# Loads of the second MoE's w_out paced by a one-column copy from the first MoE's values

## The chip, the cores and the metric

The kernel runs on one core of a Trainium2 chip. The metric is the device time of one launch in microseconds; the kernel before has a median of 1230.97 us over 3 runs (1230.19 to 1234.41). Engines are called as the profile calls them: PE is TensorE (PEld its weight loads), DVE is VectorE, ACT is ScalarE, POOL is GpSimd, and SP is the engine whose queue issues the DMAs. TensorE's clock has two levels, 1.2 and 2.4 GHz; the profile's PEclk gives the granted share of full speed.

## The reference

The program is an attention with a bias made of relative positions, followed by two MoE-like feed-forward layers:

```python
def reference(...):
    # attention: q, k, v are (4, 8, 576, 64)
    scores = q @ k^T / 8 + bias(w1, b1, w2)     # bias: relu(x @ w1 + b1) @ w2 of log distances
    attn = softmax(scores); x = (attn @ v) laid out as 2304 tokens x 512
    # first MoE, 512 -> 1536 -> 512
    g = x @ w_gate; val = x @ w_val
    x = (g * sigmoid(g) * val) @ w_out
    # second MoE, 512 -> 2048 -> 512
    h = maximum(x @ w_in, 0)
    return (h * h) @ w_out
```

The inputs that matter here are float64 weights, which the kernel decodes itself.

## The kernel before, in words

**Precision.** Matmuls run in float16. Every operand is split into a high and a low half, and a product takes three matmuls (high x high, high x low, low x high). The weights are float64 in memory: a block of 128 rows x 512 columns (512 KB) is loaded as it is, decoded on DVE into float32 by three instructions (`decode`, L262, L265, L267), its norm is taken, and once a common scale is known, each block is split into halves (`split`, `halves`): either POOL makes the high half (L197) and DVE the low one (L191), or ACT scales and casts (L205, L209) and POOL subtracts (L220).

**Two streams.** The program is written by two generators whose instructions are interleaved while it is emitted. Stream "a" holds the attention and the preparation of weights (`first`, `second`, `weights2`). Stream "m" holds the first MoE, in nine units of 256 tokens (`moe1(m)`, m = 0 to 8). Each `yield` of a number adds that much to the stream's position, and the loop at the end goes on with "m" when "a" is ahead of it by the table `LEAD`, else with "a". A scheduler with a timeline model then decides the final order on each engine.

**The first MoE.** A unit goes through 12 columns f. For each, 24 matmuls (L458) fill a PSUM tile with gate and value, ACT takes the tanh, and DVE forms `th` in two instructions (L467, L469), which also empty the PSUM tile. Three PSUM tiles are in turn (tags `mm` twice, `ma` once). ACT casts `th` to the high half of `zx`, POOL subtracts for the low half (L220). Then 2 x 36 matmuls (L481) make two output tiles of 128 tokens; `out_y` (L491 to L501) normalizes them and stores them.

**The second MoE's w_out** (key "2"). `weights2` calls `second(..., later=True)` for its 16 blocks. Three raw rooms (`w2s`) take turns. Each block is loaded by SP (L283), decoded by DVE, and its square norm goes to ACT. After each block the next load is issued into the room that came free, and the generator yields 1.6. After the last block, DVE and two small matmuls (L139 and L169) turn the norms into a scale, and the 16 splits follow one after the other. Blocks f and 8+f are then combined (`combine`, sums of L1193 and casts of L1200) for the Strassen-like products of the later units.

**The second MoE.** `plain(0)` treats unit 0 alone: layer 1 is 16 tiles of 12 matmuls (L1378), each followed by relu and square (L1383, L1387) and by the split of the result (L1198 for the cast on DVE), layer 2 is two output tiles of 48 matmuls (L1406). Five of the eight `combine` calls are written among `plain(0)`. Then come four pairs of units, (1,2) to (7,8), each with a layer 1 of 8 column steps (`hidden`: matmuls, relu and square, differences by POOL, halves) and products (`outputs`, L1450). The lines of the program are those before the change; in the changed program they stand 4 or 5 further down from the class `Source` on.

Of the kernel before, what the change touches and what calls it, by code (L numbers as in the profile page):

```python
# [10 lines left out]
F32 = mybir.dt.float32  # L11
# [5 lines left out]
ALU = mybir.AluOpType  # L17
# [58 lines left out]
def tile_attention_moe(  # L76
# [4 lines left out]
    nc = tc.nc  # L81
# [20 lines left out]
    st = {}  # L102
# [3 lines left out]
    def keep(n=1):  # L106
        sc_n[0] += 1
        return res.tile([P, n], F32, name=f"keep{sc_n[0]}")
# [3 lines left out]
    def scr(shape, dt=F32, tag="scr"):  # L112
        return small.tile(
            shape, dt, tag=who[0] + tag + "x".join(map(str, shape)), name="sc", bufs=2 if who[0] else 4)
# [71 lines left out]
    def mul(out_, a, b, f=1.0):  # L186
        nc.vector.scalar_tensor_tensor(out=out_, in0=a, scalar=f, in1=b, op0=ALU.mult, op1=ALU.mult)
# [34 lines left out]
    class Ring:  # L222


        def __init__(self, t, place):
            self.t, self.place = t, place
# [44 lines left out]
    class Source:  # L271


        def __init__(self, parts):
            self.parts, self.loaded, self.raws = parts, 0, {}

        def load(self, sg):
            if self.loaded < len(self.parts):
                key, ap = self.parts[self.loaded]
                r = self.raws[key] = sg.raw()  # L280
                n = P // len(ap)
                for i, a in enumerate(ap):
                    nc.sync.dma_start(r[n * i:n * i + n], a)  # L283
                self.loaded += 1
# [59 lines left out]
    def second(ring, key, kc_n, src, kappa, sg, ahead, mm, later=False):  # L344

        w = sg.width
        so = Source([
            ((kc, i), block_rows(src, w * i, kc, w))
            for kc in range(kc_n) for i in range(512 // w)])
        for _ in range(ahead):  # L350
            so.load(sg)
        nrm = keep(kc_n)
        for kc in range(kc_n):
            if kc == 7 and key == "o":
                yield ("kv", 8)
            f = ring.whole(key, 0, kc)
            for i in range(512 // w):
                decode(so.raws.pop((kc, i)), f[:, w * i:w * i + w])
                so.load(sg)
                yield 1.6 * w / 512  # L360
            nc.scalar.activation(
                sg.sq(), f, AF.Square, scale=kappa[kc // 4], accum_out=nrm[:, kc:kc + 1])
        m = scr([P, 1], tag="wm")
        nc.vector.tensor_reduce(out=m, in_=nrm, axis=AX, op=ALU.add)
        sc, st["i" + key] = root_scale(psum_all(m, mm), mm)
        rows = st["rows" + key] = keep(kc_n // 4)
        for j in range(kc_n // 4):
            mul(rows[:, j:j + 1], sc, kappa[j], 0.5 if later else 1.0)
        yield 1.0
        for kc in range(kc_n):  # L370
            split(ring, key, 0, kc, rows[:, kc // 4:kc // 4 + 1])
            yield 0.4
# [11 lines left out]
    def block_rows(src, c0, kc, n):  # L384
        return [src[P * kc:P * kc + P, c0:c0 + n]]
# [40 lines left out]
    def moe1(m):  # L426
# [19 lines left out]
        last = None  # L446
        for f in range(NF1):
# [16 lines left out]
            last = mw.tile([P, 256], F32, tag="th", name="th", bufs=3)  # L464
            with tc.high_priority():
                nc.scalar.activation(last, pg[:, 0:256], AF.Tanh, scale=cg)
                nc.vector.scalar_tensor_tensor(  # L467
                    out=last, in0=last, scalar=1.0, in1=pg[:, 0:256], op0=ALU.add, op1=ALU.mult)
                nc.vector.scalar_tensor_tensor(  # L469
                    out=last, in0=last, scalar=CZ, in1=pg[:, 256:512], op0=ALU.mult, op1=ALU.mult)  # L470
            f_done[0] += 1
            yield 2.6
        finish(NF1 - 1, last)
        gv_done[0] = m
# [864 lines left out]
    def mm2():  # L1339
# [4 lines left out]
        out=g2, in0=st["i2"], scalar1=2.0 / (C1 ** 2 * KR), scalar2=None, op0=ALU.mult)  # L1344
# [185 lines left out]
```

## Time and profile before

| | |
|---|---|
| median of 3 runs | 1230.97 us (1230.19 to 1234.41) |
| the profiled execution | 1225.56 us; its span 1223.8 us |
| mean granted clock of TensorE | 0.963 |
| PE busy | 1091.4 us, 89% |
| PEld, DVE, ACT, POOL busy | 807.8, 789.5, 670.6, 621.1 us (66, 65, 55, 51%) |
| the chain that ended last | PE 44%, DMA 18%, DVE 15%, POOL 10%, ACT 6%, issue 5% |

One profiled execution is a little shorter than the median of the runs; durations of single instructions come from it. A busy share is a mean over stages with different limits, so the stage from about 767 to 960 us, in which the second MoE's w_out is loaded, decoded, split and combined, is read by itself: it holds the units m = 7 and 8 of the first MoE, `plain(0)` and the first pair of the second MoE.

### The profile page before, as it was taken

The page shows a single profiled execution, that of the slowest core. Times are in us where ns is not written, and L with a number is a line of the kernel's source. Part 1 is how long each engine was busy: PE and PEld are TensorE (multiplying, and loading weights), DVE is VectorE, ACT ScalarE, POOL GpSimd, SP SyncE. Part 2 cuts the span into 40 slices and gives each one's busy share as a digit, 9 for nine tenths or more (in the row PEclk, how much of TensorE's full clock was granted, in tenths as well). Part 3 has the DMA queues.
Part 4 walks back from the last instruction along what each step waited for, and adds up shares of the span by engine and source line. Part 5 has one row for each costly group of instructions (what it writes and reads, how often), then busy time and mean ns, then how long its engine had stood idle before and what let it go on. Part 6 is the DMA issues. An engine that isn't in the chain of part 4 may idle for free.

```text
span 1223.8 us, 27145 instructions
## 1 busy us (share of the span) xinstructions
PE 1091.4 (89%) x10478; PEld 807.8 (66%) x10478; DVE 789.5 (65%) x1884; ACT 670.6 (55%) x1350; POOL 621.1 (51%) x793
## 2 busy tenths in 40 slices
PE   2588789998678989999898899979999999999998
PEld 2567688687457668687774766657744856748567
DVE  5989857797677676666675745885986344153361
ACT  3557767557567566566674454365636254262451
POOL 2433213269768587879786373225347145072350
PEclk9769799999979999999999999989999999999999
DMA  9957543229999998997989995670110202002001
GB/s 229 262 137 209 181 133 88 47 62 187 219 226 195 222 219 163 216 222 142 192 175 237 270 216 119 217 216 10 39 32 1 52 18 35 35 1 52 19 1 35
DMA packets 278078, 163.20 MB, mean 133 GB/s; under 512 B 233276, under 2 KB 246588, under 8 KB 277948
## 3 DMA queue, kind: packets, MB, share of 16 engines
q1 hardware_dynamic: 277948, 161.46, 56.4%
q8 instruction: 82, 1.34, 0.5%
q14 instruction: 48, 0.39, 0.1%
HBM read 92.13 MB, written 19.48 MB: 91 GB/s over the span
## 4 chain that ended last, share of the span: by engine, by line
PE 44%; DMA 18%; DVE 15%; POOL 10%; ACT 6%; issue 5%; SPq 2%; POOLq 0%; ACTq 0%; DVEq 0%
PE mm L458 11%; PE mm L1378 10%; PE mm L1450 10%; DMA pT<-pt 5%; POOL pt L220 3%; PE mm L481 3%; POOL zx L1193 2%; PE av L874 2%; DMA wr<-in_v_dram 2%; DMA qT<-qs 2%; PE qk L812 2%; PE ma L1450 1%; DVE w2t L1193 1%; DMA w2s<-in_moe_w_out_dram 1%; DVE scrap L604 1%
## 5 line engine op out<-in xcount | busy, mean ns | idle before, releaser
L458 PEld LDWEIGHTS <-wr 128*128 128x128 f16 x2592 | 252.1, 99 | 52.1 <-issue 17.4
L1193 POOL TENSOR_TENSOR zx<-zx 128x256 f32<-128x256 f32 x128 | 122.5, 966 | 152.7 <-ACT zx L1387 147.6
L458 PE MATMUL mm<-xT,wr 128*128 128x256 f16 x1536 | 185.4, 276 | 10.1 <-DVE th L469 6.1
L220 POOL TENSOR_TENSOR pt<-s,pt 128x512 f16<-128x512 f32 x224 | 171.3, 788 | 32.0 <-ACT pt L836 28.0
L220 POOL TENSOR_TENSOR zx<-th,zx 128x256 f16<-128x256 f32 x108 | 81.3, 754 | 125.5 <-ACT zx L443 121.7
L481 PE MATMUL mm<-wr,zx 128*128 128x512 f16 x612 | 142.1, 379 | 1.6 <-DVE th L469 1.6
L1450 PEld LDWEIGHTS <-wr 128*128 128x128 f16 x1344 | 131.3, 98 | 17.6 <-DVE wr L1198 1.0
L1193 DVE TENSOR_TENSOR wr<-zx,wr 128x768 f16<-128x768 f32 (+1 forms) x72 | 93.6, 1307 | 71.4 <-ACT wr L1200 70.4
L821 DVE CUSTOM_DVE_ANT_0 s<-qk,room 128x576 f32<-128x576 f32 x144 | 107.7, 748 | 38.0 <-PE qk L812 21.8
L829 ACT ACTIVATE s<-s,sc 128x576 f32<-128x576 f32 x112 | 85.6, 771 | 55.6 <-DVE sc L828 46.0
L458 PE MATMUL mm<-zx,wr 128*128 128x256 f16 x864 | 103.6, 276 | 3.5 <-DVE th L469 3.5
L481 PEld LDWEIGHTS <-zx 128*128 128x128 f16 x648 | 60.1, 98 | 66.1 <-issue 2.8
L604 DVE TENSOR_TENSOR scrap<-scrap,room 128x1024 f16<-128x1024 f16 (+1 forms) x108 | 87.1, 820 | 21.2 <-PE ma L643 17.6
L1378 PE MATMUL mm<-wr,w2r 128*128 128x512 f16 (+1 forms) x480 | 100.0, 358 | 0.3 <-ACT zx L1383 0.3
L1378 PE MATMUL mm<-wr,room 128*128 128x512 f16 (+1 forms) x480 | 99.9, 358 | 0.0
L620 POOL TENSOR_TENSOR scrap<-scrap 128x256 f32<-128x256 f32 (+1 forms) x90 | 64.0, 711 | 64.2 <-ACT scrap L619 56.3
L874 PE MATMUL av<-vp,pT 128*128 128x65 f16 (+3 forms) x1792 | 70.2, 196 | 27.4 <-DMA pT<-pt 23.1
L874 PEld LDWEIGHTS <-pT 128*128 128x128 f16 (+1 forms) x1792 | 61.5, 102 | 42.1 <-DMA pT<-pt 32.3
L643 PEld LDWEIGHTS <-scrap 128*128 128x128 f16 x1440 | 59.6, 104 | 29.1 <-issue 13.7
L1378 PEld LDWEIGHTS <-w2r 128*128 128x128 f16 x480 | 47.0, 98 | 47.1 <-issue 0.5
L1378 PEld LDWEIGHTS <-room 128*128 128x128 f16 x480 | 47.0, 98 | 45.8
L1469 ACT ACTIVATE ob<-ob,fac 128x256 f32<-128x256 f32 x32 | 16.0, 507 | 104.0 <-DVE ob L1468 103.9
(274 smaller groups left out, 2127.1 us busy)
## 6 DMA issues: line engine op xcount, KB each, us to landing
kp<-kT_d SPq DMA_DIRECT2D x64, 288.0 KB, 3.3
vp<-v_d SPq DMA_DIRECT2D x48, 325.0 KB, 3.6
w2s<-in_moe_w_out_dram SPq DMA_DIRECT2D x16, 512.0 KB, 4.2
wr<-in_moe_w_gate_dram SPq DMA_DIRECT2D x24, 256.0 KB, 5.2
wst<-in_moe_w_out_dram SPq DMA_DIRECT2D x12, 512.0 KB, 3.8
wr<-in_moe_w_val_dram SPq DMA_DIRECT2D x24, 256.0 KB, 4.4
v_d<-vp SPq DMA_DIRECT2D x16, 325.0 KB, 2.9
y_d<-yh SPq DMA_DIRECT2D x18, 256.0 KB, 3.3
```

Of the source, the lines that this page charges most:

```text
L220: nc.gpsimd.tensor_tensor(out=out_, in0=x, in1=hi, op=ALU.subtract)
L458: nc.tensor.matmul(pg[:, 256 * gi:256 * gi + 256], wr.parts(key, f // 4, cc, wl, P * (f % 4), P), mov(xl, cc), start=k == 0, stop=k == 11)
L481: nc.tensor.matmul(po, zall[:, f, zl, P * t:P * t + P], wr.parts("o", 0, f, wl), start=k == 0, stop=k == 3 * NF1 - 1)
L604: nc.vector.tensor_tensor(out=m[:, :, ni * e:ni * e + ni], in0=block(kb, i0, ni), in1=th, op=ALU.is_gt)
L620: nc.gpsimd.tensor_tensor(out=tmp[r], in0=tmp[r], in1=xb, op=ALU.mult)
L643: nc.tensor.matmul(pv[:, :, :, c:c + 4], m[:, a, :], bd[:, l], start=l == 0, stop=l == 1)
L821: nc.vector.tensor_tensor_reduce(out=s.rearrange("p (a j) -> p a j", a=2), in0=pq[:, :, 0:288], in1=bias[:, n].rearrange("p (a j) -> p a j ...
L829: nc.scalar.activation(s, s, AF.Exp, bias=nm, scale=-1.0)
L874: nc.tensor.matmul(av[r, slot, 0:cn], pT[:, 5 * l + c, r], vs[e][c][:, c0:c0 + cn], start=m == 0, stop=m == 13)
L1193: (nc.gpsimd if how else nc.vector).tensor_tensor(out=out_, in0=a, in1=b, op=op)
L1378: nc.tensor.matmul(ph[:, :n], w2r.parts("w", g // 4, cc, wl, P * (g % 4), P), yt[:, 4 * yl + cc, :], start=m == 0, stop=m == 11)
L1450: nc.tensor.matmul(po, HS[f][:, o:o + P], right_of(f, wl, b), start=f == 0 and k == 0, stop=f == 7 and k == 2)
```

## The change

Before each of the 16 loads of the second MoE's w_out, POOL now copies the first column of the latest `th` of the first MoE into the first column of the raw room. The load overwrites that column, so it waits for the copy, and the copy waits for `th` and for the room. The first MoE records its latest `th` in `st["th"]`. And `second` yields 3.0 instead of 1.6 after each of these blocks. The splits, the scale and the sums are untouched in themselves.

```diff
     class Source:
-        def __init__(self, parts):
-            self.parts, self.loaded, self.raws = parts, 0, {}
+        def __init__(self, parts, held=False):
+            self.parts, self.loaded, self.raws, self.held = parts, 0, {}, held

         def load(self, sg):
             if self.loaded < len(self.parts):
                 key, ap = self.parts[self.loaded]
                 r = self.raws[key] = sg.raw()
+                if self.held:
+                    nc.gpsimd.tensor_scalar(
+                        out=r.bitcast(F32)[:, 0:1], in0=st["th"][:, 0:1], scalar1=1.0, scalar2=0.0,
+                        op0=ALU.mult, op1=ALU.add)
                 n = P // len(ap)
...
         so = Source([
             ((kc, i), block_rows(src, w * i, kc, w))
-            for kc in range(kc_n) for i in range(512 // w)])
+            for kc in range(kc_n) for i in range(512 // w)], later)
...
                 decode(so.raws.pop((kc, i)), f[:, w * i:w * i + w])
                 so.load(sg)
-                yield 1.6 * w / 512
+                yield (3.0 if later else 1.6) * w / 512
...
             f_done[0] += 1
+            st["th"] = last
             yield 2.6
```

Three places show how the order of the instructions changes. The first is the start of the last unit (m = 8) of the first MoE, on DVE. Before, the rows between the `th` of f = 1 and the first `th` instruction (L467) of f = 2 of that unit; `w2r` is the ring of decoded blocks, `keep33` the scale of a block of w_in that is split here, L500 (L505 after) the low half of an output of unit 7:

```order
L500 SCALAR_TENSOR_TENSOR yh_12823<-mm_12755,sc_12820,yh_12823 128x512
L262 TENSOR_SCALAR w2r_12105<-w2s_12106 128x512
L296 COPY keep33_12437<-mm2_12435 128x1
L297 COPY keep34_12438<-mm2_12435 128x1
L267 SCALAR_TENSOR_TENSOR w2r_12105<-w2s_12106,w2r_12105 128x512
L265 SCALAR_TENSOR_TENSOR w2r_12105<-w2s_12106,w2r_12105 128x512
L187 SCALAR_TENSOR_TENSOR keep38_12518<-keep34_12438 128x1
L262 TENSOR_SCALAR w2r_12105<-w2s_12106 128x512
L191 SCALAR_TENSOR_TENSOR w2r_12105<-w2r_12105,keep33_12437 128x512
L267 SCALAR_TENSOR_TENSOR w2r_12105<-w2s_12106,w2r_12105 128x512
L265 SCALAR_TENSOR_TENSOR w2r_12105<-w2s_12106,w2r_12105 128x512
L467 SCALAR_TENSOR_TENSOR th_12953<-th_12953,mm_12926 128x256
```

After, from the `th` of f = 1 on, in the same stretch of the program on DVE:

```order
L473 SCALAR_TENSOR_TENSOR th_12865<-th_12865,mm_12838 128x256
L191 SCALAR_TENSOR_TENSOR w2r_12105<-w2r_12105,keep33_12437 128x512
L471 SCALAR_TENSOR_TENSOR th_12902<-th_12902,mm_12875 128x256
L471 SCALAR_TENSOR_TENSOR th_12939<-th_12939,ma_12912 128x256
L473 SCALAR_TENSOR_TENSOR th_12902<-th_12902,mm_12875 128x256
L473 SCALAR_TENSOR_TENSOR th_12939<-th_12939,ma_12912 128x256
L262 TENSOR_SCALAR w2r_12105<-w2s_12106 128x512
L265 SCALAR_TENSOR_TENSOR w2r_12105<-w2s_12106,w2r_12105 128x512
L191 SCALAR_TENSOR_TENSOR w2r_12105<-w2r_12105,keep33_12437 128x512
L471 SCALAR_TENSOR_TENSOR th_12971<-th_12971,mm_12944 128x256
L267 SCALAR_TENSOR_TENSOR w2r_12105<-w2s_12106,w2r_12105 128x512
L473 SCALAR_TENSOR_TENSOR th_12971<-th_12971,mm_12944 128x256
```

Before, more than two blocks are decoded between the `th` of f = 1 and that of f = 2. After, the `th` of f = 1, 2 and 3 follow each other with splits between, and the 13th block (L262) comes behind f = 3.

The copies themselves, on POOL, near the end of unit 7 (the twelve halves of `zx` that L220 makes for L481's matmuls), after the change; before it, all twelve stand in a row:

```order
L220 TENSOR_TENSOR zx<-th,zx 128x256 x9
L282 TENSOR_SCALAR w2s<-th 128x1 x2
L220 TENSOR_TENSOR zx<-th,zx 128x256
L282 TENSOR_SCALAR w2s<-th 128x1 x3
L220 TENSOR_TENSOR zx<-th,zx 128x256
L282 TENSOR_SCALAR w2s<-th 128x1 x2
L220 TENSOR_TENSOR zx<-th,zx 128x256
```

Seven copies stand among the halves of unit 7. By the names of their operands, loads 1 to 12 read a `th` of unit 7, and loads 13 to 16 the `th` of f = 1, 2, 4 and 5 of unit 8.

The second place is on PE, the root scale of w_out. Before, its first small matmul (L139) among unit 8's gate and value matmuls:

```order
L458 LDWEIGHTS wr
L458 MATMUL mm<-xT,wr 128x256
L139 MATMUL mm_12861<-ones_f,sc 1x1
L458 LDWEIGHTS wr
L458 MATMUL mm<-xT,wr 128x256
```

After, both of them (L139, L169) between unit 8's last output matmul (L486, which was L481) and the first matmul of `plain(0)` (L1383, which was L1378):

```order
L486 LDWEIGHTS zx
L486 MATMUL mm<-wr,zx 128x512
L139 MATMUL mm_13322<-ones_f,sc 1x1
L169 MATMUL mm_13333<-sc,ones_r 128x2
L1383 LDWEIGHTS room_118
L1383 MATMUL mm_13426<-wr,room_118 128x256
```

The scale, and with it all 16 splits, moves from the middle of unit 8 to its end.

The third place is layer 1 of the first pair of units, on DVE. Before, the end of the last `combine` (`w2t`) and the pair's first cast (128x768):

```order
L1193 TENSOR_TENSOR wr<-four,wr 128x1024
L1193 TENSOR_TENSOR w2t<-w2r 128x2x256
L1193 TENSOR_TENSOR w2t<-w2t,w2r 128x2x256 x2
L1193 TENSOR_TENSOR w2t<-w2r,w2t 128x256
L1193 TENSOR_TENSOR w2t<-w2t,w2r 128x256
L1193 TENSOR_TENSOR w2t<-w2r,w2t 128x256
L1193 TENSOR_TENSOR w2t<-w2t,w2r 128x256
L1198 CAST wr<-zx 128x768
L1193 TENSOR_TENSOR wr<-zx,wr 128x768
```

After (L1198 is now the sum or low half, L1203 the cast):

```order
L1203 CAST wr<-zx 128x768
L1198 TENSOR_TENSOR w2t<-w2r,w2t 128x256
L1198 TENSOR_TENSOR wr<-zx,wr 128x768
L1198 TENSOR_TENSOR w2t<-w2t,w2r 128x256
L1198 TENSOR_TENSOR wr<-zx,wr 128x1024
L1198 TENSOR_TENSOR wr<-zx,wr 128x768
L1198 TENSOR_TENSOR w2t<-w2r 128x2x256
L1198 TENSOR_TENSOR w2t<-w2t,w2r 128x2x256 x2
L1203 CAST wr<-zx 128x1024
```

The end of one `combine` and the start of another now stand behind the pair's first cast. On ACT, at the same place, before the change the pair's second PSUM tile (`mm2_13832`) follows the first directly:

```order
L1410 ACTIVATE ob_13812<-mm2_13763,fac_13406 128x512
L1383 ACTIVATE zx_101<-mm2_13817 128x512
L1387 ACTIVATE zx_101<-zx_101 128x512
L1383 ACTIVATE zx_101<-mm2_13832 128x512
L1387 ACTIVATE zx_101<-zx_101 128x512
```

After, casts of the sums (`four` to `wr`) stand between the tiles:

```order
L1415 ACTIVATE ob_13828<-mm2_13779,fac_13422 128x512
L1388 ACTIVATE zx_101<-mm2_13833 128x512
L1392 ACTIVATE zx_101<-zx_101 128x512
L1205 CAST wr_97<-four_13421 128x1024
L1388 ACTIVATE zx_101<-mm2_13848 128x512
L1392 ACTIVATE zx_101<-zx_101 128x512
L1205 CAST wr_97<-four_13421 128x1024
L1388 ACTIVATE zx_101<-mm2_13871 128x512
```

Such a cast waits for the sums of its `combine` on DVE, and the tiles behind it wait with it.

## Rows read from the trace of the kernel before

**Rows 1.** Stage window: stretch, length, busy us (instructions) per engine, PEclk, DMA share, GB/s

```profile
801.50:827.30 25.80, 17.49 (x124) 13.38 (x123) 23.63 (x62) 18.34 (x45) 6.09 (x6) 0.87 0.69 206
```

**Rows 2.** Timeline of PE, 801 to 830: start, us, what, idle before and its releaser

```profile
804.75 0.27 PE L131 MATMUL mm<-ident,sc 128*1 128x128 f32 x1 [2.29 <-DVE sc L495]
804.85 3.37 PE L458 MATMUL ma<-xT,wr 128*128 128x256 f16 x17
...
815.32 3.79 PE L458 MATMUL ma<-xT,wr 128*128 128x256 f16 x18 [4.02 <-DVE sc L166]
...
827.33 2.78 PE L458 MATMUL mm<-xT,wr 128*128 128x256 f16 x24 [1.91 <-DVE th L469]
```

**Rows 3.** Timeline of DVE, 814 to 829

```profile
814.85 0.41 DVE L469 SCALAR_TENSOR_TENSOR th<-th,ma 128x256 f32<-128x256 f32 x1
...
817.63 0.43 DVE L262 TENSOR_SCALAR w2r<-w2s 128x512 int32<-128x512 int32 x1 [1.65 <-DMA w2s<-in_moe_w_out_dram]
...
827.19 0.41 DVE L469 SCALAR_TENSOR_TENSOR th<-th,ma 128x256 f32<-128x256 f32 x1
```

**Rows 4.** Timeline of DVE, 856 to 955

```profile
856.70 0.15 DVE L147 TENSOR_SCALAR sc<-sc 128x1 f32<-128x1 f32 x1 [1.27 <-ACT junk L492]
...
904.50 0.68 DVE L1193 TENSOR_TENSOR w2t<-w2r 128x512 f32<-128x512 f16 x1
...
914.27 0.56 DVE L1198 CAST wr<-zx 128x768 f16<-128x768 f32 x1 [4.00 <-ACT zx L1387]
...
954.41 0.69 DVE L1198 CAST wr<-zx 128x1024 f16<-128x1024 f32 x1 [0.62 <-POOL zx L1193]
```

**Rows 5.** Timeline of PE, 945 to 960

```profile
955.16 0.94 PE L1450 MATMUL mm<-wr 128*128 128x256 f16 x7 [0.70 <-DVE wr L1198]
```

**Rows 6.** Groups of POOL by shape: busy us, mean ns of one, idle before

```profile
L620 POOL TENSOR_TENSOR scrap<-scrap 64x128 f32<-64x128 f32 x36 | 17.9, 497 | 1.5 <-ACT scrap L619 0.2
...
L591 POOL MEMSET room<- 128x1 f32 x5 | 0.5, 98 | 0.6 <-DVE scrap L604 0.6
```

**Rows 7.** Tile w2s: readers with ns min/median/max, first and last start; its DMAs

```profile
L262 DVE TENSOR_SCALAR w2r<-w2s x24: 404/427/1381, 767.3 to 827.9; 128x512 int32<-128x512 int32 x24
L265 DVE SCALAR_TENSOR_TENSOR w2r<-w2s,w2r x24: 668/680/1156, 767.8 to 828.8; 128x512 int32<-128x512 int32 x24
...
DMA to landing us min/median/max: 3.5/4.1/4.9
```

**Rows 8.** Timeline of PE, 846 to 960

```profile
847.83 7.93 PE L481 MATMUL ma<-wr,zx 128*128 128x512 f16 x36
...
863.37 1.26 PE L1378 MATMUL mm<-wr,w2r 128*128 128x256 f16 x10
...
894.53 11.40 PE L1406 MATMUL mm<-w2r,wr 128*128 128x512 f16 x52 [1.59 <-DVE wr L1193]
905.76 2.75 PE L1378 MATMUL mm<-wr,room 128*128 128x512 f16 x12
```

**Rows 9.** Timeline of POOL, 836 to 860: the 1st, 2nd and 5th pair of splits

```profile
838.44 0.69 POOL L197 TENSOR_SCALAR w2r<-w2r,keep 128x512 f16<-128x512 f32 x1 [0.21 <-DVE keep L187]
...
846.11 0.70 POOL L197 TENSOR_SCALAR w2r<-w2r,keep 128x512 f16<-128x512 f32 x1
...
857.41 0.69 POOL L197 TENSOR_SCALAR w2r<-w2r,keep 128x512 f16<-128x512 f32 x1
```

**Rows 10.** Groups of DVE by shape, 858.8 to 910.3

```profile
L1193 DVE TENSOR_TENSOR wr<-zx,wr 128x512 f16<-128x512 f32 x8 | 6.9, 867 | 0.3 <-ACT wr L1200 0.3
...
L1193 DVE TENSOR_TENSOR w2r<-four,w2s 128x1024 f16<-128x1024 f32 x1 | 3.1, 3145 | 0.0
...
L1193 DVE TENSOR_TENSOR w2s<-w2t,w2s 128x1024 f16<-128x1024 f32 x1 | 1.2, 1217 | 0.0
```

**Rows 11.** Groups of POOL by shape, 858.8 to 912

```profile
L1193 POOL TENSOR_TENSOR w2c<-four,w2c 128x1024 f16<-128x1024 f32 x1 | 2.5, 2543 | 0.6 <-ACT w2c L1200 0.6
```

**Rows 12.** Timeline of ACT, 985 to 1000: a tile of the second pair of units

```profile
993.17 0.60 ACT L1383 ACTIVATE zx<-mm 128x512 f32<-128x512 f32 x1 [0.53 <-PE mm L1378]
```

## Prediction

> **What bounds the kernel now.** I read the chain that ended last, then the stages in windows, then engine timelines where TensorE (PE) stands still. The chain runs mostly over PE, so PE's work sets the end, and what the chain spends elsewhere are holes in that work. One hole lies where the change works. From 801.5 to 827.3 us PE is busy 17.49 of 25.80 us at a mean granted clock of 0.87, while DVE is busy 23.63 [rows 1]: 8.3 us idle, and 0.13 x 25.8 = 3.4 us lost to the lower of the clock's two levels. There PE begins the last unit (m=8) of the first MoE, and DVE decodes w_out's blocks between the instructions that empty PE's PSUM tiles. PE waits 2.29 us for a scalar of DVE, then 4.02 us, then 1.91 us for th [rows 2]. (The 4.02 us are put down to a scalar, but f=0's L469 starts at 814.85 and lasts 0.41 [rows 3]; its end at 815.26 frees the PSUM tile that the matmul of 815.32 writes.) After the first two waits PE is at the lower clock: 17 matmuls in 3.37 us and 18 in 3.79 instead of some 0.11 us each.
>
> From 863.4 us on PE has almost no holes. The second MoE has a tight place all the same: in the first unit pair's layer 1, ACT, GpSimd (POOL) and DVE turn each PSUM tile into halves for the product, and the last such cast, at 954.41 [rows 4], makes PE wait 0.70 us at 955.16 [rows 5]. There is no spare time there.
>
> **The change part by part.**
>
> *The copies.* Sixteen POOL instructions of one column. The trace has none. Bounds from rows: a one-column memset 98 ns, a 64x128 tensor_tensor 497 ns [rows 6]; I take 0.1 us, since the size is that of the memset. 1.6 us of an idle POOL in all, nothing on PE's path by themselves. Each is a wait, though. Behind it in POOL's order stand halves of zx that L481's matmuls read: the 10th half of unit 7 now follows two copies, the 11th five and the 12th seven. I take 0, since DVE's decode of the block three before frees each room and stands in DVE's own order ahead of those halves' use. Bounds: 0, since a copy gives PE nothing, and 1.5, one block's decode, if a copy finds its room still undecoded. The values that the copies read are old for the first twelve loads, so only four of sixteen loads are held by anything but their rooms. This narrows what the change does, and is in the sum.
>
> *A. Unit 8's start, 801.5 to 827.3.* Before f=0's L469, the old DVE order has twelve blocks' first instructions, the new eleven. A block is one instruction of 0.43 and two of 0.68 us [rows 7], 1.55 us in a row, since each begins before the one ahead is out, so th of f=0 comes some 1.6 us sooner, at 813.7. PE gets there sooner too (no wait of 2.29, no slow 17 matmuls), but gains only what DVE gains: one wait of 6 us instead of two. The slow 18 matmuls stay. Then f=2 and f=3: their L469 now stand before blocks 13 to 15. DVE needed 12.3 us from f=0's L469 to f=3's (814.85 to 827.19, with a DMA wait of 1.65 [rows 3]); the new rows between them (one block and the last third of another, yh, two splits, six th instructions, at 0.4 to 0.75 us each) add up to about 7.2. So the 1.91 us wait goes. Reckoned to PE's start of f=5, the tile at 827.33: f=3's tile starts at 813.7 and takes 4.4 us (18 of its 24 matmuls 3.79 as before [rows 2], the last six 0.11 each), f=2 and f=4 take 2.6 each, so f=5 starts at 823.3, 4.0 earlier. I take 0.6 back for blocks 13 to 16, whose loads now start only after th of f=1, 2, 4 and 5 and, on the SP queue, after unit 0's transpose, with 4.1 us to landing [rows 7]. Together -3.4. Bounds: -11.7, the whole hole (8.3 + 3.4), and +2, if the four held loads land as late as 4.9 us and DVE's order makes th wait behind them.
>
> *B. The root scale.* Its two small matmuls (L139, L169) stood among unit 8's matmuls and were hidden. Now they stand behind its last L481, and the DVE chain between them also holds a copy that waits for ACT's square of the last output tile. In the trace such a tile ended at 847.83 + 7.93 = 855.76 [rows 8] and that L147 started at 856.70 [rows 4]: 0.94; four more small instructions make PE idle some 1.25 us. Bounds 0.6 and 2.5 (the latter if the clock falls; after the waits of 1.91 and 1.59 us [rows 2, 8] the matmuls ran at full speed).
>
> *C. Plain unit 0.* The splits of w_out start only now, so they run beside this unit's layer 1 (21 us) and layer 2 (21 us) instead of ahead of it. Block 8, which layer 2 needs first, belongs to the 5th pair of splits. The first pair started at 838.44, the second at 846.11, the 5th at 857.41 [rows 9]: the first takes 7.7 us because ACT scales eight blocks in it, the others 3.8. ACT now has unit 0's tiles between them, so I take 4.4 (an estimate): the 5th at T + 2.5 + 7.7 + 3 x 4.4 = T + 23.4, with T the end of the last L481. PE reaches layer 2 at about T + 22.7, takes two output tiles in turn and needs 2.6 us per column step; pairs deliver two steps in 4.4. No wait to speak of, and the old 1.59 and 0.31 us (DVE was busy with sums for the later units) go: -1.9. Bounds -1.9 and +2.
>
> *D. The first pair's layer 1.* The eight combine() sums need blocks f and 8+f, so none can start before the 5th pair of splits. Before, that pair started at 857.41 and PE's first matmul of the unit pair at 905.76 [rows 8]: 48.3 us. After, plain unit 0 takes PE from T to T + 43.4 (863.37 to 905.76 less 1.9 of waits, plus 14 matmuls that stood earlier, plus B), so only 20 us lie between. From 857.41 to the pair's first cast at 914.27 DVE worked 52.9 us (56.9 less a wait of 4.00 [rows 4]). In the new order one combine (from 904.50 [rows 4] to 910.3, the end of [rows 10]'s stretch: 5.8) and the end of another (0.5) stand behind that cast; ahead of the 5th pair stand most of unit 0's eight low halves and three casts (some 6.3 of 6.9 [rows 10] and 0.8) and, by estimate, 3.3 of a split, yh and small scalars. 36.2 are left, with 1.5 of waits for the splits: the cast comes at T + 61.1, that is 17.7 after PE's first matmul of the pair where it was 8.5: 9.2 later. ACT's order says the same: the second PSUM tile of the pair now stands behind the cast of a combine(). On POOL two more low halves of 2.5 us [rows 11] now stand among the pair's differences: another 2.5 once its idle gaps are filled. What is given back? The old loop ran 40.14 us from first to last cast against PE's 41.4, so hardly anything; in the second pair ACT waits for PE (0.53 us [rows 12]), so the work alone would be shorter. I credit 3.1 of 41. PE's wait grows by 9.2 + 2.5 - 3.1 = 8.6. Bounds -0.7 (all caught up, and the old 0.70 gone) and +11.7 (nothing caught up).
>
> One row weighs on D: the same DVE subtraction took 1217 ns in one place and 3145 ns in another [rows 10], where a POOL half ran beside it. The Trainium skill, SBUF — State Buffer, section "Who interferes with whom", has a DVE instruction with two SBUF inputs and a GpSimd instruction that reads SBUF block each other for the whole instruction. I used the old stretch's own mixture; by the rule, the two POOL halves that now meet hidden-layer work of DVE would cost it up to 5 us, and the sum would be some 2 us worse.
>
> Sum: -3.4 + 1.25 - 1.9 + 8.6 = +4.55 us. The profiled execution took 1225.56 us (span 1223.8 and 1.8 around it), so 1230.1 there; it ran 5.4 below the median of 1230.97, on which the same difference gives 1235.5.
>
> **The rivals.** About 0.3% (3.7 us) is what a measurement of this kernel can tell from no change.
>
> *Same.* The elementwise loop catches up by 0.9 us in each of eight column steps, 7.2 us. For it: ACT's waits for PE in later pairs. Against it: first to last cast took 40.14 us with PE's data nearly always there. Then D is 4.5, the sum +0.4: 1231.4.
>
> *Faster.* DVE is out of PE's way at unit 8's start: f=0's th is there when PE ends f=1 (some 807 us), the whole hole of 11.7 closes and the clock holds. It decides if DVE gets through eleven blocks some 6 us sooner than I count, for instance because it loses its DMA waits. With D at 6.5: -11.7 + 1.25 - 1.9 + 6.5 = -5.8: 1225.2. Against it: eleven of twelve blocks still stand before th of f=0.
>
> *Much slower.* A closed loop: th, copy, load, decode, and the next th behind that decode in DVE's order. With 4.9 us to landing instead of 3.5 [rows 7], 1.4 x 4 held loads = some 6 us on PE: 1241.5. Against it: three PSUM tiles are in flight.
>
> **How the numbers follow.** The forecast holds 0.37, same 0.33, faster 0.20, much slower 0.10. So slower by over 0.3% has 0.47. The likeliest case's own range is 1232 to 1239; the range that leaves out about 2 in 10 runs from 1226 (into the faster case) to 1242.
>
> **What would show it.** Right: PE idle about 6 us once between 800 and 815 instead of twice; L139 and L169 right behind the last L481 with 1 to 1.5 us between; no long wait in unit 0; a wait of 5 to 11 us of PE at the first pair's product, for a DVE cast or subtraction; from the second pair on the same times, shifted. Wrong: if that wait is under 3 us, or PE is busy through 800 to 815, or PE waits repeatedly for th between 820 and 840.

## The result, and the profile after

The changed kernel is slower: 1252.36 us (1247.69 to 1255.59, 6 runs) against 1232.69 us (1230.19 to 1237.18, 6 runs), a ratio of 1.0144, 95% interval 1.012 to 1.0167, which is some 17.8 us (the two medians differ by 19.7). The forecast was +4.5 us; the sign is right, the size is not, and the time lies outside the range of 1226 to 1242.

The two profiled spans (1251.5 and 1223.8 us) differ by 27.7 us, but 11.3 of these arise before any changed instruction: unit 7 of the first MoE starts at 758.01 us after and at 746.71 before, and up to there every engine has the same instructions in the same order. So the traces are compared by stages that begin at unit 7's start, read off PE's timeline (us; "unit 8 to the pair" holds unit 8 and plain unit 0):

| stage | before | after | change |
|---|---|---|---|
| unit 7, gate and value | 38.46 | 38.64 | +0.2 |
| unit 7, output tiles | 16.35 | 19.21 | +2.9 |
| unit 8 to the first pair | 104.24 | 100.55 | -3.7 |
| first pair, layer 1 | 41.44 | 51.09 | +9.7 |
| first pair, products | 37.94 | 45.42 | +7.5 |
| second pair to the end | 238.64 | 238.62 | 0.0 |

The sum is +16.5 us, near the 17.8 of the timed runs. The loss lies in the first pair, and some of it at unit 7's end. The windows of the changed kernel for unit 8's start (the stretch that answers to [rows 1]) and the pair's two stages (stretch, length, busy us per engine, PEclk, DMA share, GB/s):

```profile
815.86:837.45 21.59, 15.05 (x124) 12.68 (x123) 16.73 (x49) 12.87 (x32) 7.58 (x10) 0.84 0.56 153
916.41:967.50 51.09, 43.61 (x194) 19.15 (x193) 41.99 (x47) 28.40 (x41) 39.24 (x28) 0.97 0.03 11
967.50:1012.92 45.42, 39.85 (x338) 33.59 (x337) 14.99 (x22) 10.59 (x18) 9.49 (x10) 0.92 0.15 36
```

Before, the pair's two stages were these:

```profile
905.76:947.20 41.44, 41.44 (x193) 18.80 (x192) 25.88 (x24) 26.19 (x40) 29.56 (x29) 1.00 0.02 7
947.20:985.14 37.94, 37.20 (x337) 32.63 (x336) 10.74 (x18) 7.31 (x13) 5.31 (x6) 1.00 0.17 43
```

Within the pair's layer 1 DVE is busy 16 us longer and POOL 10 us longer than before, and PE, which had no hole there, stands idle for 7.5 us. PE's timeline after, from unit 7's outputs to the products (before: [rows 2, 5, 8]):

```profile
805.37 4.17 PE L486 MATMUL mm<-wr,zx 128*128 128x512 f16 x18 [1.47 <-ACT zx L447]
...
825.18 4.08 PE L462 MATMUL mm<-xT,wr 128*128 128x256 f16 x24 [6.54 <-DVE sc L147]
...
864.58 7.93 PE L486 MATMUL mm<-wr,zx 128*128 128x512 f16 x36
...
873.86 0.35 PE L169 MATMUL mm<-sc,ones_r 1*128 1x2 f32 x2 [1.23 <-DVE sc L157]
874.14 1.48 PE L1383 MATMUL mm<-wr,room 128*128 128x256 f16 x12
...
895.12 21.46 PE L1411 MATMUL mm<-w2r,wr 128*128 128x512 f16 x96
916.41 2.75 PE L1383 MATMUL mm<-wr,room 128*128 128x512 f16 x12
...
942.05 2.75 PE L1383 MATMUL mm<-wr,w2r 128*128 128x512 f16 x12 [2.16 <-ACT zx L1388]
...
963.39 4.31 PE L1383 MATMUL mm<-wr,w2r 128*128 128x512 f16 x12 [2.02 <-ACT zx L1388]
...
978.56 0.61 PE L1455 MATMUL ma<-w2r,wr 128*128 128x256 f16 x2 [3.80 <-ACT wr L1205]
```

Unit 8's start has one long wait, of 6.54 us, where it had two, as forecast; the 24 matmuls behind it take 4.08 us instead of 2.78, at a granted clock of 0.67 in that stretch. Layer 2 of plain unit 0 (895.12) has no wait. The pair waits four times already in layer 1 (two of the four rows stand here), and then 5.6 us in four pieces for the halves of its products.

The pair's layer 1 is a loop of eight column steps. Of its casts to high halves DVE makes every third; the first of them belongs to the first step and the last to the last, so they mark the loop's length. These are the pair's first, second and last cast on DVE, after (before: [rows 4]):

```profile
932.78 0.55 DVE L1203 CAST wr<-zx 128x768 f16<-128x768 f32 x1
...
947.62 1.21 DVE L1203 CAST wr<-zx 128x1024 f16<-128x1024 f32 x1
...
980.68 0.69 DVE L1203 CAST wr<-zx 128x1024 f16<-128x1024 f32 x1 [0.62 <-POOL zx L1198]
```

Counted from PE's first matmul of the pair (916.41), the first cast comes at 16.4 us, where it came at 8.5: 7.9 later. From first to last cast the loop takes 47.9 us, where it took 40.1: 7.8 more, of which 6.2 lie between the first cast and the second. Together 15.6 of the 17.1 us; the other 1.5 stand behind the last cast, where PE ran at a granted clock of 0.50 for the first 3.3 us (980.68 to 984.00) and had 1.00 before. Up to the first cast DVE is the engine without a gap: it is busy 16.34 of the 16.37 us. Behind that cast nine instructions of the sums on DVE (6.4 us), three low halves of the sums on POOL (6.4 us) and two of their casts on ACT (2.1 us) stand in the loop, and none of these stood there before. How the tiles are held up, in rows of ACT and of POOL:

```profile
928.88 1.04 ACT L1205 CAST wr<-four 128x1024 f16<-128x1024 f32 x1 [6.91 <-DVE four L1198]
929.83 0.59 ACT L1388 ACTIVATE zx<-mm 128x512 f32<-128x512 f32 x1
```

```profile
931.16 5.11 POOL L1198 TENSOR_TENSOR zx<-zx 128x256 f32<-128x256 f32 x2 [5.74 <-ACT zx L1392]
936.22 2.12 POOL L1198 TENSOR_TENSOR wr<-four,wr 128x1024 f16<-128x1024 f32 x1
...
972.11 3.98 POOL L1198 TENSOR_TENSOR zx<-zx 128x256 f32<-128x256 f32 x4 [1.63 <-ACT zx L1392]
```

ACT stands 6.9 us before the cast of a sum that DVE has not finished, with the pair's second tile behind it. POOL gets that tile late, takes 2.5 us each for two differences that take 1.0 each later in the loop (972.11), and then makes a low half of a sum.

The loss at unit 7's end: the second instruction of the last `th` (f = 11) on DVE, before and after.

```profile
790.62 0.40 DVE L469 SCALAR_TENSOR_TENSOR th<-th,ma 128x256 f32<-128x256 f32 x1
```

```profile
807.81 0.41 DVE L473 SCALAR_TENSOR_TENSOR th<-th,ma 128x256 f32<-128x256 f32 x1
```

From unit 7's start that is 43.9 us and 49.8 us. On DVE two more blocks are decoded between the `th` of f = 9 and of f = 10:

```profile
796.04 0.41 DVE L473 SCALAR_TENSOR_TENSOR th<-th,mm 128x256 f32<-128x256 f32 x1
798.52 0.43 DVE L262 TENSOR_SCALAR w2r<-w2s 128x512 int32<-128x512 int32 x1 [0.33 <-DMA w2s<-in_moe_w_out_dram]
801.04 0.43 DVE L262 TENSOR_SCALAR w2r<-w2s 128x512 int32<-128x512 int32 x1 [0.45 <-DMA w2s<-in_moe_w_out_dram]
802.11 0.41 DVE L471 SCALAR_TENSOR_TENSOR th<-th,mm 128x256 f32<-128x256 f32 x1
```

### The profile page after: what moved, and what is told of

Read it like the earlier page. It is cut to its first block, busy times and chain, and to the rows that moved or that the text cites. A ratio compares the mean times of both kernels' runs of the same rounds, so it can differ in the third digit from the quotient of the medians.

```text
span 1251.5 us, 27180 instructions
## 1 busy us (share of the span) xinstructions
PE 1099.5 (88%) x10478; PEld 811.2 (65%) x10478; DVE 793.2 (63%) x1884; ACT 670.0 (54%) x1350; POOL 632.5 (51%) x809
## 5 line engine op out<-in xcount | busy, mean ns | idle before, releaser
L1198 POOL TENSOR_TENSOR zx<-zx 128x256 f32<-128x256 f32 x128 | 127.4, 1005 | 155.9 <-ACT zx L1392 149.9
L220 POOL TENSOR_TENSOR pt<-s,pt 128x512 f16<-128x512 f32 x224 | 173.2, 796 | 32.9 <-ACT pt L841 28.6
L486 PE MATMUL mm<-wr,zx 128*128 128x512 f16 x612 | 143.7, 382 | 2.7 <-ACT zx L447 1.5
L220 POOL TENSOR_TENSOR zx<-th,zx 128x256 f16<-128x256 f32 x108 | 79.2, 734 | 119.1 <-ACT zx L447 115.1
L1198 DVE TENSOR_TENSOR wr<-zx,wr 128x768 f16<-128x768 f32 (+2 forms) x72 | 94.1, 1317 | 70.4 <-ACT wr L1205 69.5
L1383 PE MATMUL mm<-wr,w2r 128*128 128x512 f16 (+1 forms) x480 | 101.5, 362 | 5.6 <-ACT zx L1388 5.6
L486 PEld LDWEIGHTS <-zx 128*128 128x128 f16 x648 | 60.3, 98 | 68.8 <-issue 4.3
L1383 PE MATMUL mm<-wr,room 128*128 128x512 f16 (+1 forms) x480 | 99.9, 358 | 1.9 <-ACT zx L1388 1.9
L1383 PEld LDWEIGHTS <-w2r 128*128 128x128 f16 x480 | 47.3, 99 | 53.2 <-issue 7.9
L1383 PEld LDWEIGHTS <-room 128*128 128x128 f16 x480 | 46.9, 98 | 47.8 <-issue 2.2
L817 PE MATMUL qk<-kp,qT 128*128 128x288 f16 x384 | 63.8, 292 | 10.6 <-DMA kp<-kT_d 6.6
```

The source lines that it names most:

```text
L220: nc.gpsimd.tensor_tensor(out=out_, in0=x, in1=hi, op=ALU.subtract)
L486: nc.tensor.matmul(po, zall[:, f, zl, P * t:P * t + P], wr.parts("o", 0, f, wl), start=k == 0, stop=k == 3 * NF1 - 1)
L817: nc.tensor.matmul(pq[:, j, 0:288], qT[:, 2 * (n % 4) + s, :], kts[0][:, js], start=s == 0, stop=s == 1)
L1198: (nc.gpsimd if how else nc.vector).tensor_tensor(out=out_, in0=a, in1=b, op=op)
L1383: nc.tensor.matmul(ph[:, :n], w2r.parts("w", g // 4, cc, wl, P * (g % 4), P), yt[:, 4 * yl + cc, :], start=m == 0, stop=m == 11)
```

## The experiments

My theory, P: the pace (the number that `second` yields after each block) costs, since it puts the scale and the splits behind unit 8, so that DVE's sums run into the first pair, whose loop can't make that up. Rivals are named where they are tried.

All stages are from the profile of each run, counted as above; "sum" is unit 7's start to the second pair against before, and the ratio is of the timed runs, against runs of the kernel before taken with them, with its interval. "Copies" are the one-column copies.

| run | unit 7 outputs | unit 8 to pair | pair, both stages | sum | ratio |
|---|---|---|---|---|---|
| before | 16.35 | 104.24 | 79.38 | 0 | 1 |
| after | 19.21 | 100.55 | 96.51 | +16.5 | 1.0144 (1.012 to 1.0167) |
| e1 copies alone | 22.85 | 104.51 | 79.41 | +6.9 | 1.0044 (1.0013 to 1.0075) |
| e2 pace alone | 16.35 | 103.98 | 96.30 | +16.8 | 1.0124 (1.0083 to 1.0165) |
| e3 copies, pace 2.6 | 20.25 | 103.61 | 84.10 | +7.7 | 1.0063 (1.0032 to 1.0094) |
| e4 after, short sums | 18.38 | 99.47 | 85.12 | +3.4 | 1.0026 (0.9993 to 1.0058) |
| e5 after, copies on DVE | 18.23 | 103.12 | 97.17 | +18.4 | 1.0117 (1.0083 to 1.0152) |
| e6 after, difference on DVE | 18.58 | 100.05 | 95.09 | +13.5 | 1.0115 (1.0077 to 1.0153) |
| e7 after, halves on DVE | 18.26 | 99.31 | 93.81 | +10.9 | 1.0103 (1.0084 to 1.0122) |
| e8 copies on DVE, pace 1.6 | 22.40 | 99.15 | 82.41 | +3.8 | 1.0019 (0.9992 to 1.0045) |
| e9 copies for loads 9 to 16, pace 1.6 | 16.35 | 102.66 | 83.49 | +2.5 | 1.0012 (0.9987 to 1.0037) |
| e12 copies for loads 13 to 16, pace 1.6 | 16.35 | 100.90 | 83.87 | +1.0 | 0.9999 (0.9977 to 1.0022) |
| e14 as e12, unit 0's low halves on POOL | 16.35 | 110.48 | 78.28 | +4.8 | 1.0047 (1.0025 to 1.0068) |
| e15 before, unit 0's low halves on POOL | 16.35 | 108.41 | 79.15 | +4.1 | 1.0027 (1.0002 to 1.0053) |
| e11 before, splits off DVE | 16.75 | 104.21 | 78.12 | -0.5 | 0.9974 (0.9951 to 0.9997) |

In e10 and e13 PE takes a matmul or more of the pair inside unit 0's layer 2, so unit 8 and the pair can't be parted: 199.4 and 200.8 us together, against 183.6 before and 197.1 after.

**e1 and e2, one half of the change each.** e1 keeps the copies, e2 the pace:

```diff
e1  -                yield (3.0 if later else 1.6) * w / 512
    +                yield 1.6 * w / 512
e2  -            for kc in range(kc_n) for i in range(512 // w)], later)
    +            for kc in range(kc_n) for i in range(512 // w)])
```

> The copies stay, the pace is 1.6 again: the decodes are held as in the changed kernel, but the root scale stands among unit 8's matmuls and the splits ahead of plain unit 0. Theory P (the late splits cost the time: in the changed kernel's profile 9.7 us in the first pair's layer 1 and 7.5 in its product, while unit 7's end to the pair's start came out 0.6 us ahead): the time is that of before less 1.3 us (3.1 gained at unit 8's start, 1.8 lost to the copies at unit 7's end), so -4 to +1 us against before. Rival H (the hold costs it, by loads that come late and halves that queue behind copies on POOL): +8 to +18 us against before.

> The copies go, the pace of 3.0 stays: the decodes stand as in the kernel before, the root scale and the splits as in the changed kernel. Theory P: +14 to +20 us against before, PE waits some 17 us in the first pair, and the hole of some 12 us at unit 8's start is there as before. Rival H: within 4 us of before.

e2 bears theory P out: the pace alone gives nearly the whole loss in the pair (16.9 of 17.1 us), and its casts stand at the same distances as after. The first and the last cast of DVE in e2, 47.90 us apart again:

```profile
930.09 0.55 DVE L1203 CAST wr<-zx 128x768 f16<-128x768 f32 x1
...
977.99 0.69 DVE L1203 CAST wr<-zx 128x1024 f16<-128x1024 f32 x1 [0.62 <-POOL zx L1198]
```

e1 misses both expectations: the pair is untouched, but the copies cost 6.5 us at unit 7's end, and give nothing at unit 8. The 3.7 us that the changed kernel gains ahead of the pair thus come from neither half alone: that stage takes 104.51 us in e1 and 103.98 in e2. PE at unit 7's end, in e1:

```profile
810.98 6.65 PE L486 MATMUL mm<-wr,zx 128*128 128x512 f16 x18 [3.63 <-DVE th L473]
```

**e3, how the cost follows the pace.** With the copies, 2.6 for 3.0.

> The copies stay, the pace is 2.6 instead of 3.0: the root scale's matmuls stand in unit 8 again, two columns later than at 1.6, and the splits ahead of plain unit 0. Theory P: -4 to +2 us against before, for at unit 8's start the decodes stand as in the changed kernel, and nothing of the 17 us in the first pair is lost. A rival G (the cost grows with the pace, block by block): two thirds of the loss stays, +10 to +14 us.

Neither: layer 1 of the pair is at its old 41.44 us, so the jump comes between 2.6 and 3.0, but the products still take 4.7 us more. The cost grows neither evenly nor in one step.

**e4, DVE's sums shortened in the changed kernel.** In `combine` the instructions that take in the low halves are left out (four of the seven, not three of six as the expectation counted), so the sums are of the high halves alone:

```diff
         diff(t13, right(0), left(0), mixed("t"))
-        diff(t13, t13, right(1), mixed("t"), ALU.add)
-        diff(t13, t13, left(1), mixed("t"))
...
             diff(x, q[:, c], y, mixed("t"))
-            diff(x, x, q[:, c + 2], mixed("t"), ALU.add)
```

> The changed kernel with three of the six DVE instructions of each combine() left out (the sums are then not those of the reference). DVE's share of a combine falls from 5.8 us to about 2.9, 23 us less in all. If the first pair is late because DVE reaches the sums late and everything behind waits in order (theory P's mechanism): 10 to 16 us faster than the changed kernel, so +1 to +8 us against before. If POOL's halves in the pair's loop are what costs (rival), DVE's 23 us bring under 5 us: +13 to +18 us.

As theory P has it: the pair gets back 11.4 of its 17.1 us. The first and last cast:

```profile
922.47 0.56 DVE L1203 CAST wr<-zx 128x768 f16<-128x768 f32 x1 [3.18 <-ACT zx L1389]
...
962.59 0.69 DVE L1203 CAST wr<-zx 128x1024 f16<-128x1024 f32 x1 [0.61 <-POOL zx L1198]
```

The loop is back at 40.12 us, to 0.02 us what it took before. The first cast still comes 12.9 us after the pair's start (909.60) instead of 8.5, and those 4.4 us are not made up in eight column steps. What e4 does not part is DVE's sums from the work that follows them: with shorter sums, their casts and POOL's low halves stand ahead of the first cast too, and nothing of them is left in the loop.

**e5, the copies on DVE.**

```diff
-                    nc.gpsimd.tensor_scalar(
+                    nc.vector.tensor_scalar(
                         out=r.bitcast(F32)[:, 0:1], in0=st["th"][:, 0:1], scalar1=1.0, scalar2=0.0,
```

> The changed kernel with the one-column copies on DVE instead of POOL. Theory Q (the copies cost by standing in POOL's order ahead of zx's halves: unit 7's output stage takes 19.2 us in the changed kernel, 22.9 with the copies alone, 16.35 before): the stage falls back to 16.3 to 17 us and the whole is 2 to 3 us faster than the changed kernel, +14 to +16 us against before. Rival L (the loads themselves come late, wherever the copy stands): the stage stays at 19 us, the whole at +17 to +19 us.

Theory Q falls by the stage: unit 7's end stays at 18.23 us, next to the 18.3 to 19.7 of the kernels that have all copies on POOL at this pace, and does not come near 16.35. (The timed difference, some 14.5 us, is one that Q expects, but its interval, 10 to 19 us, takes in both.) That the copies stand in POOL's order is not the main cost.

**e6, e7 and e10, other engines' work in the pair.** In the changed kernel, one difference in four, all low halves of the sums, or the high casts of the sums go to DVE (in the table of engines, 0 is DVE):

```diff
e6   -"s": (1,)          +"s": (1, 1, 1, 0)
e7   -"d": (0, 1, 1)     +"d": (0,)
e10  -"c": (1,)          +"c": (0,)
```

> The changed kernel with one of the four differences of each column step of the later pairs on DVE instead of POOL. Theory R (the pair's elementwise loop has no slack, since POOL's four differences and the waits around them fill 5.25 us of each column step against PE's 5.18; a late start is never made up): a step gets up to 0.8 us shorter, so 4 to 6 us of the 17 come back, +12 to +14 us against before. Rival (DVE, late with the sums, is what holds the loop, and one more instruction there costs more): no gain or a loss, +17 to +21 us.

> The changed kernel with all eight low halves of the sums on DVE instead of three on DVE and five on POOL. If POOL's halves inside the pair's loop cost (two of 2.1 us each among the differences, and the differences beside DVE's sums 2.5 us instead of 1.0): 3 to 6 us faster than the changed kernel, +12 to +15 us against before. If DVE's sums alone are the path (theory P): five more instructions of 1.2 us there, 2 to 6 us slower, +19 to +24 us.

> The changed kernel with the high casts of the sums on DVE instead of ACT. In the changed kernel ACT stands 6.9 us before such a cast while two PSUM tiles of the first pair wait behind it, and PE then waits 9.7 us in that layer 1. If that place in ACT's order is the cost (theory A): the 9.7 us of layer 1 fall to under 5 and the whole is 4 to 8 us faster than the changed kernel, +10 to +14 us against before. If the lateness of DVE's sums is (theory P): DVE has eight more casts of some 0.7 us, the product waits longer by what layer 1 waits less, and the whole stays at +15 to +21 us.

e6 comes out at +14.2 us and e7 at +12.7, at the edge of and within what their theories of POOL expect, but the stages tell that apart: of the 3.0 and 5.6 us that the two gain on the changed kernel, 1.4 and 2.7 lie in the pair. In e7 the first cast comes 12.1 us after the pair's start instead of 16.4, and the loop takes 48.8 us instead of 47.9. So taking these off POOL is worth 1.4 and 2.7 of the 17.1 us, net of what they then cost on DVE, and theory P's expectation of a loss in e7 was wrong. In e7 the loop is long with no half of the sums on POOL and 13.6 us of sums on DVE in it: POOL's halves are not needed for the loss. e10 gives theory A none of the gain that it expects: without the casts on ACT, layer 1 waits in another place (PE, e10):

```profile
952.61 5.13 PE L1383 MATMUL mm<-wr,w2r 128*128 128x512 f16 x12 [5.64 <-ACT zx L1388]
...
968.55 0.40 PE L1455 MATMUL ma<-w2r,wr 128*128 128x256 f16 x1 [3.77 <-DVE wr L1198]
```

At the first of these rows ACT had stood 7.28 us for differences of POOL. The ratio of e10 is 1.015 (1.011 to 1.0189). DVE gets eight more casts by this edit, so a smaller share of ACT's order is not ruled out.

**e8, e9 and e12, a hold that should cost nothing.** e8 is e5 at the pace of 1.6. e9 and e12 have the copies on POOL, the pace of 1.6 and

```diff
-                if self.held:
+                if self.held and self.loaded >= 8:      # e9; e12: >= 12
```

> Copies on DVE and the pace of 1.6. By theories P and Q nothing is left that costs: unit 7's output stage takes 16.4 us, the splits stand ahead of plain unit 0, and the first pair is as before; what is left is what the held decodes give at unit 8's start, 0 to 4 us: -4 to +1 us against before. By rival L: +4 to +8 us, as with the copies on POOL at this pace (+5.4).

> Copies (on POOL) only before loads 9 to 16, and the pace of 1.6. Theory C (a closed loop in DVE's order: with the first loads held, the last th of unit 7 stand behind decodes of blocks whose loads wait for the th before; unit 7's output stage grew from 16.35 to 18.2 to 22.9 us in every kernel with all loads held, on POOL or DVE alike): with the first eight loads free, unit 7's th stand as before and its stage takes 16.4 us; unit 8's gate and value stage gains 1 to 4 us, the first pair is as before. In all -4 to 0 us against before. Rival (a copy costs wherever it stands): the stage stays above 18 us, +2 to +6 us.

> Copies only before loads 13 to 16, pace 1.6: the four loads that in the changed kernel read a th of unit 8. Theory C: unit 7's stage 16.4 us; by the order of DVE the th of f = 1 to 3 now stand ahead of the last four decodes, so unit 8's stage gains 1 to 3 us: -3 to 0 us against before. Rival: within 1 us of before, since the decodes' sum on DVE is the same and only its order moved.

e9 and e12 bear out what theory C says of unit 7: with the first eight loads free, its stage is 16.35 us to the hundredth, and PE runs through it:

```profile
806.46 3.61 PE L486 MATMUL mm<-wr,zx 128*128 128x512 f16 x16
```

That row is e9's, the last of the stage, and has no wait. Unit 8 to the pair gains 1.6 us in e9 and 3.3 in e12. But the pair takes 4.1 and 4.5 us more, since its first cast comes 11.5 us after its start in both, and the loop then takes 40.12 and 40.13. So e9 and e12 come out the same as before, and theory C's expectation that the pair stays as it was is missed. Why that cast is 3 us later, though in e12 the splits begin 35.9 us after unit 8's start and before 36.9, was not isolated. e8 misses: unit 7's stage is at 22.4 us, as in e1.

**e11, DVE relieved in the kernel before.** ACT and POOL alone (2) split the last eight blocks of w_in:

```diff
-"w": (0, 1, 2)
+"w": (0, 1, 2, 0, 1, 2, 0, 1, 2, 2, 2, 2, 2, 2, 2, 2)
```

> The kernel before, with the last eight splits of w_in made by ACT and POOL alone, so that DVE has five instructions of 0.74 us less between 790 and 840 us. If DVE's work is what PE waits for at unit 8's start: 2 to 4 us less in unit 8's gate and value stage (46.3 us before), -4 to -1 us in all. If the wait for loads is: no change, -1 to +1 us.

The timed runs fit the first expectation (some 3.2 us less), but the interval ends just below 1, the profile shows only 0.5 us, and the gain expected in unit 8 is not there (104.21 us). It is the only one of fifteen tried kernels whose interval lies below 1, and with so many tries that can be chance; a gain is not shown. PE still stands for DVE at unit 8's start:

```profile
827.79 0.56 PE L169 MATMUL mm<-sc,ones_r 1*128 1x2 f32 x2 [4.05 <-DVE sc L166]
```

**e13, e14 and e15, DVE relieved in plain unit 0.** Its eight low halves go to POOL, in the changed kernel, in e12 and in the kernel before (the new key "E" is (1,), POOL):

```diff
-            parts2(h[:, 0:512], h[:, 512:1024], x, "a", "e")
+            parts2(h[:, 0:512], h[:, 512:1024], x, "a", "E")
```

> The changed kernel with the eight low halves of plain unit 0 on POOL instead of DVE (6.9 us of DVE's work before). Theory P (DVE's sums set the first pair): the pair's first cast comes some 6 us earlier relative to the pair's start, its loop keeps part of its 7.8 us: 6 to 10 us faster than the changed kernel, +8 to +12 us against before. Rival S (the splits' chain, which starts only after the scale, sets it): POOL, which makes splits too, gets slower, and the whole stays at +15 to +20 us.

> Copies before loads 13 to 16 only, pace 1.6, and plain unit 0's low halves on POOL. Theory P: unit 8's start to the pair's start keeps its 3 us (100.9 instead of 104.2), the pair's cast is not late any more, its layer 1 and product take 78.5 to 80 us: -3 to -6 us against before. Rival S: layer 1 and product stay at 83 to 84 us, -1 to +1 us in all.

> The kernel before, with plain unit 0's low halves on POOL. Theory P: the waits of 1.59 us in unit 0's layer 2 and 0.70 us in the pair go, -2 to -1 us, for the pair's loop has nothing else to give (its first to last cast take 40.14 us against PE's 41.4). Rival S: no change, -0.5 to +1 us.

e13 comes out as rival S expects, at 1.0157 (1.0118 to 1.0196); e14 and e15, at 1.0047 and 1.0027, are worse than either expectation. So in the changed kernel taking this work off DVE gives nothing back, against theory P, and e13 leaves open how much of the lateness is the splits' chain, in which POOL works too. The pair does get faster where the splits are early (78.3 us in e14, 79.2 in e15), but unit 8 to the pair grows to 110.5 and 108.4 us, since PE's layer 2 now waits for halves on POOL (e15):

```profile
900.17 3.03 PE L1406 MATMUL mm<-w2r,wr 128*128 128x512 f16 x12 [0.84 <-POOL wr L1193]
```

So this work of DVE can't be put on POOL for free, and e14's gain in the pair (5.6 us against e12) cost 9.6 ahead of it.

## Why the prediction was too small

**The base** was right: the profiled execution before was a short one, and differences had to be put on the median. The spread in front of unit 7 is the reason (its start lay between 746.1 and 761.6 us in these profiles).

**The copies, taken at 0, bounds 0 and 1.5.** Wrong: 2.9 us at unit 7's end. I looked for the price in POOL's order and took the first twelve loads to be held by nothing but their rooms. e5 shows that the place in POOL's order is not the main cost; e9 shows that holding the first eight loads is what costs. By the rows above the price is in DVE's order, where two more decodes now stand ahead of the `th` of f = 10 and 11; no run changes that order alone. I had compared DVE's order at unit 8's start and not at unit 7's end. The rival of a closed loop (th, copy, load, decode, next th) named the decode ahead of the next th, but put it into unit 8, where it did not come. That the copied value itself holds the loads is not what the trace shows: of POOL's idle time just before the sixteen copies, 10.6 us in six waits ended with a decode (L267) and 3.6 us in one wait with a `th` (L473). A copy took 0.21 us in the median, where I had 0.1.

**A, B and C: -3.4 + 1.25 - 1.9 = -4.05; measured -3.7.** Right, and in the way described: one wait of 6.54 us (about 6 forecast), no wait for th of f = 3, 1.63 us from the last output matmul's end (872.51) to plain unit 0 (874.14; 1.25 forecast), no long wait in unit 0.

**D, +8.6; measured +17.1.** This is the step that failed, in one term. The first cast was forecast 9.2 us late and came 7.9 us late: right. "What is given back?" was answered with -3.1, and POOL's added halves with +2.5: the loop was to be 0.6 us shorter. It is 7.8 us longer. The sign that I named, a wait of 5 to 11 us at the pair's product, came with 5.6 us, but PE lost another 7.5 in layer 1, where I had it run without a wait. The row for ACT's waits in the second pair [rows 12] suggested spare time, but in that pair ACT waits for PE, so PE paces the loop. In the first pair, where no sums stand inside it, the loop takes 40.1 us however late it starts: 40.14 before and 40.16 in e1 (first cast 8.5 us after the pair's start), 40.12 in e9 and 40.13 in e12 (11.5 us), 40.12 in e4 (12.9 us). (e3, e11 and e14, also without sums in it, take 40.5 to 40.9; the last two start earliest, at 6.7 us.) From 8.5 us on it has no slack, so no lateness comes back. In the seven kernels where sums stand inside it (the changed one, e2, e5, e6, e7, e10, e13), it is 7.1 to 8.7 us longer. I took the combine that moved behind the first cast as time saved ahead of it (5.8 + 0.5 us), and did not charge it behind; 6.4 us of DVE's sums stood there. The upper bound of +11.7, "nothing caught up", still left the loop at its old length but for 2.5 us of POOL; so the range ended too low.

**The rule on DVE and POOL.** Two differences on POOL beside DVE's sums took 5.11 us (931.16), where four took 3.98 behind the last sum (972.11). The Trainium skill, SBUF — State Buffer, section "Who interferes with whom", says that a DVE instruction with two SBUF inputs contends with a GpSimd instruction that reads SBUF; the trace agrees, 1.5 us for each of these two. How much of the 17.1 us is such contention, and how much the time of the sums themselves, no run here parts. e7 does not: it takes the low halves off POOL and gains 2.7 us in the pair, but leaves the differences beside DVE's sums, where five of them take 14.26 us (e7):

```profile
915.87 14.26 POOL L1198 TENSOR_TENSOR zx<-zx 128x256 f32<-128x256 f32 x5 [10.27 <-ACT zx L1392]
```

**The cause, then.** The pace of 3.0 puts the last decode, and with it the scale and all splits, at the end of unit 8. DVE's sums then run into the first pair, delay its first cast by 7.9 us and stand in its loop for another 7.8. That the pace does it is shown by e2, and by e1, where the pair is untouched without it. That the sums do it is shown by e4: with DVE's part of them shortened, 11.4 of the 17.1 us come back. How much of the first cast's lateness the late splits themselves make is open (e13), and so is which engine's share of the sums lengthens the loop: moving halves, differences or casts between POOL, ACT and DVE (e6, e7, e10) gains 2.7 us at most in the pair. The copies add 2.9 us at unit 7's end; together with the pace they bring the 3.7 us gained after it, which in e1 they don't bring.

## What to carry to other kernels

Before a late start is credited with catching up, look for a second stretch of the same loop: if it takes the same time whatever its start, it has no slack, and work moved into it is to be charged there (here 6 to 14 us of DVE's sums in the loop made it 7 to 9 us longer). A wait that is added to a load moves more than the load: compare the order of every engine that consumes it, from the first load on and not only where the change aims. And compare two traces by stages from a common point, since the part in front can differ by more than the change.

## What was not expected of the hardware

Late stages repeat to some hundredths of a microsecond where the order is the same (unit 7's outputs 16.35 us in six profiles, the second pair to the end 238.62 to 238.67 in all seventeen), while the part in front of unit 7 took 746.1 to 761.6 us, though all seventeen kernels have the same instructions there in the same order. What makes that part vary was not looked into.
